# Splitting the first load and the first backward scan of a recurrent attention kernel's boot in two

## The chip, the core and the metric

The kernel runs on one core of a Trainium2 chip. The core has four engines that compute, each with its own list of instructions: TensorE (PE in the profile; PEld is its loading of weights), VectorE (DVE), ScalarE (ACT) and GpSimd (POOL). SyncE (SP) issues most of the DMAs, which move data between the chip's memory and the core's. The metric is the device time of the whole kernel in microseconds, as a median over runs.

## What is computed

The reference is a recurrent attention (RWKV-6) and, on its result, a two-layer network with the activation h - tanh(h):

```python
for t in range(S):                      # B, H, S, D = 4, 8, 768, 48
    kt, vt, rt, wt = (k[:, :, t], v[:, :, t], r[:, :, t], w[:, :, t])
    cur = np.einsum('bhd,bhe->bhde', u[None] * kt, vt)
    y[:, :, t] = np.einsum('bhd,bhde->bhe', rt, state + cur)
    state = wt[:, :, :, None] * state + np.einsum('bhd,bhe->bhde', kt, vt)
x = y.transpose(0, 2, 1, 3).reshape(B * S, H * D)
h = x @ w_in                            # 384 -> 2048
g = h - np.tanh(h)
out = g @ w_out                         # 2048 -> 384
```

The decay w lies between 0.8 and 0.95, one factor for every position and feature. All inputs are float32.

## The kernel before

**Tiles.** The work is cut into eight blocks of 384 positions (four batches, two blocks each). A block has six chunks of 64 positions. The eight heads go in four pairs (numbered 0 to 3); a pair of heads fills the 128 partitions with their features (48 of each 64 used), and positions run along the columns. In w each chunk has 65 columns: a leading one and 64 positions, so a pair of one block has 6 x 65 = 390 columns, and two pairs, a "half" of a block, have 780. The half with pairs 2 and 3 comes first (`h1` in the code), that with pairs 0 and 1 second (`h2`).

**The recurrence as matrix products.** Within a chunk the decay between two positions is a product of w's. Two scans on VectorE make these products. `behind` (line 420, its instruction recorded at line 429) runs backward over w and writes the tile `post`: at each position the product of all decays from there to the end of its chunk. The columns run in reverse, and at the leading column of each chunk the tile `seed` holds a 1, which restarts the product. `before` (line 413, scan at line 417) runs forward and writes `pre`. `take_whole` (line 449) takes the total decay of each chunk out of `post`, and the reciprocal at line 416 turns it over for `before`. Then k is multiplied into `post` (line 443) and r into `pre` (line 436); TensorE forms the scores within a chunk (line 494) and the turned keys (line 517); VectorE copies the scores under a mask (line 502); line 616 gives what each chunk adds to the state, line 631 scans the states over the chunks, and lines 697 and 679 give the attention's result from scores and states.

**The boot.** The first block can hide behind nothing, and `boot` (line 1128) does it by itself, with an order written out by hand: the instructions of TensorE, SP, VectorE and ScalarE stand in the order of the calls. SP issues first the loads: w of pair 3, w of pair 2, k and r of the first half, w of the second half, v, k and r of the second half, then the first two units of the network's weights. For the first block, w is put into the tile `states` (`states0`), so the profile calls these loads `states<-in_wT`. Then VectorE runs `behind` for pair 3 alone, for pair 2 alone, the totals, `before` and the products for the first half, and `behind` for the second half in one scan of 780 columns. TensorE meanwhile does matmuls on an identity matrix whose results nobody reads (lines 305 and 312; `spare=94, ahead=5, late=6` says how many). ScalarE multiplies u into k (line 454), copies results out of PSUM (lines 523, 729) and rebuilds the weights from the two words that each is stored in (line 264, VectorE's part at line 268).

**After the boot** comes the main loop: for each block sixteen steps of the first layer's product (`first`, line 869; matmuls at line 871), the activation and the second layer (lines 950 and 999), with the next block's attention in between. TensorE is handed this work without a break until the end.

**Order of the queues.** SP issues in the order of the calls. Each DMA reports on one of eight semaphores in turn, and its issue waits until the DMA eight before it has landed. The second unit of weights waits besides until line 616 is done.

Of the kernel before, what the change touches and what calls it, by code (L numbers as in the profile page):

```python
# [55 lines left out]
NCH = NB // L  # L56
NCP = NCH // 2
NPAIR = H // 2
LP = L + 1
WIDE = NPAIR * NCH * LP  # L60
HALF = WIDE // 2 + 2
UP = 2
# [64 lines left out]
def kernel(  # L127
# [12 lines left out]
    nc = tc.nc  # L140
# [46 lines left out]
    def draw(names, cols):  # L187
        nc.gpsimd.memset(mask_all[0:L, cols], 1.0)
        for m in names:
# [5 lines left out]
            else:  # L195
# [10 lines left out]
                   in_=start[:, 0:BANK].unsqueeze(1).to_broadcast([P, 2 * NPAIR * NCP * L // BANK, BANK]))  # L206
# [113 lines left out]
    class Block:  # L320
# [40 lines left out]
        def load(self, name, p0=0, n=NPAIR, as_=None):  # L361
# [4 lines left out]
            else:  # L366
# [2 lines left out]
            return nc.sync.dma_start(out=dst.rearrange("d (p t) -> d p t", p=n),  # L369
                                     in_=src.rearrange("p d t -> d p t"))  # L370

        def by_token(self, name):

            return self.tile(name)[:, 0:NCP * DM].rearrange("t (c e) -> t c e", c=NCP)
# [42 lines left out]
            return nc.vector.tensor_tensor_scan(out=self.tile("pre")[:, cols], data0=self.tile("w")[:, cols],  # L417
                                                data1=start[:, 0:n * NCH * LP], initial=0.0, op0=ALU.mult, op1=ALU.add)

        def behind(self, p0, n):  # L420
            a, width, at = p0 * NCH * LP, n * NCH * LP, p0 % UP * NCH * LP
            t = self.half("post", p0, at + width + 1)[:, at:]
            if at + width == UP * NCH * LP:
                nc.gpsimd.memset(t[:, width:], 1.0)

            def back(x):
                return x[:, ::-1]

            return nc.vector.tensor_tensor_scan(  # L429
                out=back(t[:, 0:width]), data0=back(self.tile("w")[:, a:a + width]),  # L430
                data1=back(seed[:, 0:width]), initial=1.0, op0=ALU.mult, op1=ALU.max)
# [696 lines left out]
    def boot(ps, pair, blk, later):  # L1128
        h1, h2 = HALVES
        blk.tiles["w"] = states0  # L1130
        for name, p0, n in (("w", h1 + 1, 1), ("w", h1, 1), ("k", h1, UP), ("r", h1, UP), ("w", h2, UP)):
            blk.load(name, p0, n)
        blk.load_v()
        blk.load("k", h2, UP)
# [1 line left out]
        more_weights(nc.sync)  # L1136

        both = (h1, h1 + 1), (h2, h2 + 1)
        blk.behind(h1 + 1, 1)
        blk.behind(h1, 1)  # L1140
        blk.take_whole(h1, UP)
        blk.totals_by_column(h1)
# [72 lines left out]
    with tc.tile_pool(name="ps_boot", bufs=1, space=PSUM) as ps_boot:  # L1215
        pieces = boot(Turns([scratch(ps_boot)] + ps_a.both), [hp] + acc, blocks[0], blocks[1])
    ps_d = mains.enter_context(tc.tile_pool(name="ps_d", bufs=1, space=PSUM))
    acc += [ps_d.tile([P, BANK], F32, name=f"acc{j}", tag=f"acc{j}") for j in range(1, NB // P)]
    count = const.tile([P, 1], F32, name="count", tag="count")
    ahead_of_h, rest, formed, extra, behind, due, summed = [], [], [], [], [], [], []  # L1220
    held_back, forming, late = [], [], []

# [24 lines left out]
    for i, blk in enumerate(blocks):  # L1247
# [9 lines left out]
        for f in range(NF):  # L1257
# [21 lines left out]
            if not now:  # L1279
                ops = square + converting(pieces, 2)  # L1280
            elif now == 1:
                ops = rest + late + square + converting(pieces, 3)
            elif not i:
                ops = extra + square + (rest + behind + spare if f < 7 else rest[:1] + behind + spare + rest[1:])
            elif forming:
                ops = between(rest, forming[:2]) + square + formed + forming[2:]
                ops = (between(ops, behind) if len(behind) > 2 else ops + behind) + spare
            elif square:
                ops = (between(rest, behind) if len(behind) > 2 else rest + behind) + square + formed + extra + spare
            else:  # L1290
                ops = between(rest + formed, behind + spare)
            for op in ops:
                op()
            rest, behind, formed, forming, held_back = later_ops, [], [], held_back, []
# [23 lines left out]
            if not later and f == NF - 2:  # L1318
                at = n_whole + n_excess
# [29 lines left out]
            for name in loads.get(f, ()):  # L1349
                of, ins = (after if name in ("w", "k", "r") else later), None  # L1350
# [103 lines left out]
```

## Time and profile before

| | us |
|---|---|
| median of 3 runs | 544.92 |
| lowest and highest | 544.65, 544.99 |
| the profiled execution | 545.84 |
| its span, first to last instruction | 544.1 |
| TensorE busy | 533.7 |
| VectorE busy | 459.0 |
| ScalarE busy | 403.8 |

The mean granted clock of TensorE was 0.995 of the full one. The profiled execution has its own time, 545.84, which holds the span and 1.7 us around it. Start times in the profile count from the first instruction. A busy time is the sum of an engine's instructions. The chain that ended last is followed back from the last instruction to what released it, step by step; only what is on it sets the time. A DMA has two times: how long SP was busy with its issue, and how long it was from the issue to the landing of its last byte.

### The profile page before, as it was taken

How to read it: one execution, taken by the hardware profiler on the slowest of the kernel's cores; microseconds unless marked ns; L12 is line 12 of the kernel's file. 1: busy time of each engine (PE TensorE's matmuls, PEld its weight loads, DVE VectorE, ACT ScalarE, POOL GpSimd, SP SyncE). 2: the span in 40 equal slices, each digit the busy share in tenths (PEclk: the TensorE clock that was granted, in tenths of full speed). 3: DMA queues.
4: the chain of work that ended last, by engine and by line, in shares of the span. 5: the costliest groups of instructions: out<-in, count | busy, mean ns of one | idle time of the engine just before them, and what ended most of it. 6: DMA issues, size and time to landing. Idle time of an engine off the chain costs nothing.

```text
span 544.1 us, 14866 instructions
## 1 busy us (share of the span) xinstructions
PE 533.7 (98%) x5682; PEld 404.1 (74%) x5682; DVE 459.0 (84%) x943; ACT 403.8 (74%) x814; POOL 6.6 (1%) x47
## 2 busy tenths in 40 slices
PE   7899999999999999999999999999999999999996
PEld 5756666678887788777877787877878787787874
DVE  7889999999989989789897979879897997457564
ACT  5799996888668876688676886588866885666561
POOL 1100000000000000000000000000000000000000
PEclk9899999999999999999999999999999999999999
DMA  7798633251402631154212532137231420200101
GB/s 274 236 400 308 237 102 115 87 146 60 121 19 79 159 110 54 58 128 138 60 55 73 121 116 67 49 89 161 67 97 54 92 56 2 57 1 0 45 1 46
DMA packets 53048, 56.34 MB, mean 104 GB/s; under 512 B 21488, under 2 KB 50928, under 8 KB 52976
## 3 DMA queue, kind: packets, MB, share of 16 engines
q1 hardware_dynamic: 52592, 55.18, 33.8%
q8 instruction: 48, 0.79, 0.6%
q14 instruction: 24, 0.20, 0.1%
q10 hardware_dynamic: 288, 0.10, 0.1%
q0 software_dynamic: 96, 0.07, 0.1%
HBM read 44.73 MB, written 4.72 MB: 91 GB/s over the span
## 4 chain that ended last, share of the span: by engine, by line
PE 95%; DVE 2%; issue 1%; DMA 0%; PEld 0%; PEldq 0%; DVEq 0%; SPq 0%
PE hp L871 44%; PE acc L999 26%; PE att L999 7%; PE acc L950 5%; PE att L757 4%; PE att L494 2%; PE acc L977 2%; PE att L575 1%; PE att L871 1%; PE acc L871 1%; DVE post L429 1%; DVE scores L502 1%; DMA states<-in_wT 0%; DVE pre L417 0%; PE att L977 0%
## 5 line engine op out<-in xcount | busy, mean ns | idle before, releaser
L871 PE MATMUL hp<-xT,w_sb 128*128 128x384 f32 x738 | 259.2, 487 | 0.4 <-DVE w_sb L268 0.4
L871 PEld LDWEIGHTS hp<-xT,w_sb 128*128 128x128 f32 x738 | 131.9, 190 | 69.7 <-issue 0.5
L999 PE MATMUL acc<-forms,g 128*128 128x128 f32 x954 | 133.2, 276 | 0.0
L876 ACT ACTIVATE h<-hp 128x384 f32<-128x384 f32 x123 | 60.4, 491 | 97.3 <-PE hp L871 97.1
L999 PEld LDWEIGHTS acc<-forms,g 128*128 128x128 f32 x954 | 122.0, 192 | 10.3
L879 DVE SCALAR_TENSOR_TENSOR h<-h,s 128x384 f32<-128x384 f32 x128 | 70.5, 551 | 50.5 <-ACT s L894 50.4
L920 DVE TENSOR_TENSOR g<-g 128x256 f32<-128x256 f32 x265 | 103.1, 418 | 7.3 <-PE acc L999 6.5
L895 ACT ACTIVATE qa<-s,shift 128x384 f32<-128x384 f32 x113 | 69.5, 615 | 3.7
L897 ACT ACTIVATE junk<-s,shift 128x384 bf16<-128x384 f32 x113 | 67.7, 599 | 0.0
L879 DVE SCALAR_TENSOR_TENSOR g<-qa,h 128x384 f32<-128x384 f32 x112 | 61.6, 550 | 1.6 <-ACT qa L905 0.2
L894 ACT ACTIVATE s<-h 128x384 f32<-128x384 f32 x113 | 59.1, 523 | 3.5
L999 PEld LDWEIGHTS acc<-w_sb,g 128*128 128x128 f32 x318 | 46.8, 191 | 9.7 <-ACT sums L967 0.3
L999 PE MATMUL acc<-w_sb,g 128*128 128x128 f32 x318 | 53.1, 276 | 0.0
L999 PE MATMUL att<-w_sb,g 128*128 128x128 f32 x212 | 35.5, 275 | 0.0
L999 PEld LDWEIGHTS att<-w_sb,g 128*128 128x128 f32 x212 | 31.1, 192 | 5.3
L1034 DVE TENSOR_TENSOR sums<-sums 128x256 f32<-128x256 f32 x84 | 32.8, 406 | 1.7 <-ACT sums L1011 1.5
L950 PE MATMUL acc<-w_sb,sums 128*128 128x384 f32 x96 | 33.7, 487 | 0.0
L264 ACT ACTIVATE up<-raw 128x768 f16<-128x768 f32 (+1 forms) x32 | 33.1, 1069 | 0.0
L950 PEld LDWEIGHTS acc<-w_sb,sums 128*128 128x128 f32 x96 | 18.0, 190 | 12.3 <-DVE sums L879 0.3
L417 DVE TENSOR_TENSOR_SCAN pre<-w,start 128x780 f32<-128x780 f32 x14 | 25.0, 1783 | 0.8
L429 DVE TENSOR_TENSOR_SCAN post<-w,seed 128x780 f32<-128x780 f32 x14 | 24.8, 1774 | 0.0
L897 ACT ACTIVATION_READ_ACCUMULATOR junk<-s,shift 128x1 f32 x113 | 21.1, 187 | 0.0
(118 smaller groups left out, 529.2 us busy)
## 6 DMA issues: line engine op xcount, KB each, us to landing
raw<-in_weights SPq DMA_DIRECT2D x16, 768.0 KB, 5.9
w<-in_wT SPq DMA_DIRECT2D x7, 780.0 KB, 4.6
k<-in_kT SPq DMA_DIRECT2D x7, 768.0 KB, 4.6
r<-in_rT SPq DMA_DIRECT2D x7, 768.0 KB, 4.6
v_sb<-in_v SPq DMA_DIRECT2D x8, 576.0 KB, 3.9
k<-in_tokens SPq DMA_DIRECT2D x7, 576.0 KB, 5.2
r<-in_tokens SPq DMA_DIRECT2D x7, 576.0 KB, 4.7
out_y<-sums SPq DMA_DIRECT2D x18, 128.0 KB, 1.8
```

The source lines that it names most:

```text
L264: return lambda: nc.scalar.activation(out=to, in_=of, func=AF.Copy, scale=scale, bias=bias)
L429: return nc.vector.tensor_tensor_scan(out=back(t[:, 0:width]), data0=back(self.tile("w")[:, a:a + width]), data1=back(seed[:, 0:width]), i ...
L871: nc.tensor.matmul(hp, lhsT=w_in_sb[:, f, kc, :], rhs=xT[kc], start=(kc == KC - 1), stop=(kc == 0))
L876: return h, nc.scalar.activation(out=h, in_=hp, func=AF.Copy, scale=1.0 / UPSCALE)
L879: return lambda: nc.vector.scalar_tensor_tensor(out=out, in0=in0, scalar=scalar, in1=in1, op0=op0, op1=ALU.mult)
L894: nc.scalar.activation(out=s, in_=h, func=AF.Square)
L895: nc.scalar.activation(out=qa, in_=s, func=AF.Square, bias=shift[:, 4:5])
L897: nc.scalar.activation(out=junk[:, 0:NB], in_=s, func=AF.Relu, bias=shift[:, 5:6], accum_out=excess[:, at:at + 1])
L920: return lambda: nc.vector.tensor_tensor(out=G[:, to:to + 2], in0=two(G, g_at(q, a0), g_at(q, a1)), in1=two(G, g_at(q, b0), g_at(q, b1)), ...
L950: nc.tensor.matmul(acc, lhsT=g[:, j * P:(j + 1) * P], rhs=w_out_sb[:, f, :], start=(f == self.first), stop=(f == NF - 1))
L999: nc.tensor.matmul(to, lhsT=G[:, g_at(q, a), :], rhs=rhs, start=start, stop=stop, skip_group_check=True)
L1034: ops.append(lambda op=op, at=at: nc.vector.tensor_tensor(out=at[0], in0=at[1], in1=at[2], op=OPS[op]))
```

## The change

The load of w for pair 3 is replaced by two loads of 195 columns each: first chunks 3 to 5 of that pair, then chunks 0 to 2. The backward scan of pair 3, one instruction of 390 columns, becomes two of 195 in the same order (the scan runs backward, so the later chunks come first). Everything else keeps its order. SP has one DMA more ahead of all other loads, VectorE one scan more. Lines behind the change move: 429 becomes 434, 449 becomes 454, 502 becomes 507, 697 becomes 702 and so on; the new loads are on line 374.

```diff
+        def load_chunks(self, p, chunks):
+            at, of = (slice((n + chunks.start) * LP, (n + chunks.stop) * LP) for n in (p * NCH, self.q * NCH))
+            return nc.sync.dma_start(out=self.tile("w")[:, at], in_=wT[self.b, p, :, of])
...
-        def behind(self, p0, n):
-            a, width, at = p0 * NCH * LP, n * NCH * LP, p0 % UP * NCH * LP
+        def behind(self, p0, n, chunks=slice(0, NCH)):
+            first, last = (p0 * NCH + c for c in (chunks.start, (n - 1) * NCH + chunks.stop))
+            a, width, at = first * LP, (last - first) * LP, first % (UP * NCH) * LP
...
     def boot(ps, pair, blk, later):
         h1, h2 = HALVES
         blk.tiles["w"] = states0
-        for name, p0, n in (("w", h1 + 1, 1), ("w", h1, 1), ("k", h1, UP), ("r", h1, UP), ("w", h2, UP)):
+        parts = slice(NCP, NCH), slice(0, NCP)
+        for part in parts:
+            blk.load_chunks(h1 + 1, part)
+        for name, p0, n in (("w", h1, 1), ("k", h1, UP), ("r", h1, UP), ("w", h2, UP)):
             blk.load(name, p0, n)
...
-        blk.behind(h1 + 1, 1)
+        for part in parts:
+            blk.behind(h1 + 1, 1, part)
         blk.behind(h1, 1)
```

## The prediction

> **What bounds the kernel now.** I read the page first: the totals and the chain that ended last.
>
> ```profile
> span 544.1 us, 14866 instructions
> ...
> PE 533.7 (98%) x5682; PEld 404.1 (74%) x5682; DVE 459.0 (84%) x943; ACT 403.8 (74%) x814; POOL 6.6 (1%) x47
> ...
> PE 95%; DVE 2%; issue 1%; DMA 0%; PEld 0%; PEldq 0%; DVEq 0%; SPq 0%
> ```
>
> TensorE holds 95% of the chain. The change adds nothing to it, so only what starts TensorE's long run earlier or later can count. Hence the second view: the chain in order of time, first 40 us (start, length, what).
>
> ```profile
> 0.94 2.60 DMA states<-in_wT
> ...
> 3.64 1.84 DVE post L429 x2
> ...
> 7.77 0.32 DVE post L443
> ...
> 8.62 0.95 DVE pre L436
> ...
> 12.31 0.16 DVE post L443
> ...
> 13.17 1.03 DVE scores L502
> ...
> 14.24 0.59 PEld att L697 x36
> ...
> 25.02 4.98 PE acc L871 x12
> 30.01 1.94 PE hp L871 x6
> ```
>
> Here the change sits on the path: the chain begins with the first load of w (tile `states`), goes on with the two backward scans of line 429, and stays on VectorE until line 697 hands it to TensorE. A tenth gained or lost there is a tenth of the whole, if nothing between takes it back. What could take it back are the other loads of the boot, so the third view is SP's timeline (start, length of the issue), and behind it the time from issue to landing: by tile, w then k then r, minimum/median/maximum, and then one row for each load.
>
> ```profile
> 0.94 0.87 SPq L369 DMA_DIRECT2D states<-in_wT  x2
> 1.86 0.43 SPq L369 DMA_DIRECT2D k<-in_kT  x1
> 2.33 0.48 SPq L369 DMA_DIRECT2D r<-in_rT  x1
> 2.85 0.47 SPq L369 DMA_DIRECT2D states<-in_wT  x1
> 3.37 0.48 SPq L406 DMA_DIRECT2D v_sb<-in_v  x1
> 3.89 0.76 SPq L369 DMA_DIRECT2D k<-in_kT  x1
> 4.69 0.92 SPq L369 DMA_DIRECT2D r<-in_rT  x1
> 5.65 8.21 SPq L251 DMA_DIRECT2D raw<-in_weights  x2
> ```
>
> ```profile
> DMA to landing us min/median/max: 2.6/2.7/6.2
> ...
> DMA to landing us min/median/max: 5.2/6.7/8.1
> ...
> DMA to landing us min/median/max: 5.7/7.0/8.3
> ```
>
> ```profile
> raw<-in_weights SPq DMA_DIRECT2D x1, 768.0 KB, 9.2
> v_sb<-in_v SPq DMA_DIRECT2D x1, 576.0 KB, 7.6
> ...
> u_sb<-in_uT ACTq DMA_DIRECT2D x1, 2.0 KB, 2.2
> ```
>
> Start plus landing time gives: pair 3 of w 0.94 + 2.6 = 3.54; pair 2 of w 1.39 + 2.7 = 4.09 (its issue is the second of the two in 0.87 us); k 7.06; r 8.03; w of the second half 2.85 + 6.2 = 9.05; v 10.97; k of the second half 3.89 + 8.1 = 11.99; r of the second half 12.99; the first weights 5.65 + 9.2 = 14.85. The first scan starts at 3.64, 0.10 after its load: that is the price from landing to start. It does not wait for pair 2, so a scan waits for its own load alone.
>
> **The front end, step by step.** The rows for a scan's length and for the rate of transfer (the window row reads: length, busy time of the engines, clock, DMA share, GB/s):
>
> ```profile
> L429 DVE TENSOR_TENSOR_SCAN post<-states,seed x3: 944/971/1775, 3.6 to 9.5; 128x390 f32<-128x390 f32 x2, 128x780 f32<-128x780 f32 x1
> ```
>
> ```profile
> 2.50:3.50 1.00, 1.00 (x47) 1.00 (x44) 0.00 (x0) 0.99 (x3) 0.64 (x3) 1.00 0.99 347
> ```
>
> - Landing of a half. 195 KB land in 2.6, 2 KB in 2.2. The ends for 97.5 KB are these two; in the middle lies 2.4, which I take. The first half lands at 3.34, its scan starts at 3.44: a lead of 0.20 (0 to 0.40).
> - Scan of 195 columns. From 390 to 780 columns it costs 1775 - 944 = 831 ns more, 2.13 ns a column; so 195 columns cost 944 - 415 = 0.53 us, between half of 944 (0.47) and 944. The line through two rows is near the lower end, so I take 0.53. The halves together are 1.06 where one scan had 0.92 of the chain (1.84 / 2): 0.14 of the lead is gone.
> - Second half. An issue slot is (2.33 - 0.94) / 3 = 0.46. Issued at 1.40, landed at 3.80, usable at 3.90; the first scan ends at 3.97. No wait.
> - Pair 2. This is the step the lead dies on. Its load is now third, at 0.94 + 2 x 0.46 = 1.87. With the best landing time of a load its size, 2.6, it lands at 4.47 and its scan starts at 4.57. The two halves are done at 3.44 + 1.06 = 4.50. Before, the same scan started at 3.64 + 0.92 = 4.56. So the pair of scans ends at 4.57 + 0.92 = 5.49, where it was 5.48: the front end gives nothing, +0.01. A half's issue could be shorter than a slot; no row shows a load of w of such size, and the two k issues, one size, took 0.43 and 0.76, so I leave it a slot. If the issues of both halves fit in one slot, and the lead is 0.40, and the halves cost 0.92 together, the scans end at 5.08: -0.40.
>
> The Trainium skill, "DMA: Bandwidth & Descriptors", section "Anatomy of one DMA", speaks against halving: about 2.0 us of a DMA are fixed and only bytes over 436 GB/s scale, for DMAs issued from GpSimd. By it a half would land 0.23 earlier, an estimate from that page, beside my 0.20; the rows 2.2 and 2.6 agree with it, and the sum would not move.
>
> **The queue behind it.** Every later load of the boot is issued one slot (0.46) later. What of this reaches the landing? At 347 GB/s 195 KB (199,680 bytes) take 0.575 us. Before, two w loads kept the queues busy for 1.15, longer than their two slots (0.93): k started 1.15 after the first byte. After, the pair 2 load has its slot at 0.93 and is done at 1.50; three slots are 1.39. So k, and all behind it, comes 1.50 - 1.15 = 0.35 later (bounds: 0, if the later backlog swallows the hole, and 0.57, below). What each load has to spare is read from these rows (VectorE's, TensorE's and ScalarE's timeline):
>
> ```profile
> 9.49 1.77 DVE L429 TENSOR_TENSOR_SCAN post<-states,seed 128x780 f32<-128x780 f32 x1
> ...
> 11.39 1.02 DVE L502 COPY_PREDICATED scores<-mask_all,att 128x768 f32<-128x768 uint8 x1
> ```
>
> ```profile
> 12.19 0.25 PE L616 MATMUL hp<-v_sb,ks 64*64 64x48 f32 x1
> ```
>
> ```profile
> 14.98 0.90 ACT L264 ACTIVATE w_sb<-raw 128x768 f32<-128x768 f32 x1
> 16.54 0.97 ACT L729 COPY late<-att 48x384 f32<-48x384 f32 x2 [0.66 <-PE att L679]
> ```
>
> - k is used at 7.77, has 7.77 - 7.06 - 0.10 = 0.61 to spare; r at 8.62, 0.49; w of the second half at 9.49, 0.34; v at 12.19, 1.12. Three are covered for 0.35, and the w load is even (0.01 late).
> - k of the second half is used at 12.31, where VectorE comes from the scores of 11.39 (no wait now): spare 12.31 - 11.99 - 0.10 = 0.22. **Here 0.35 - 0.22 = 0.13 comes out.** Queued behind that product on VectorE is the masking copy at 13.17, and line 697 on TensorE waits for that.
> - r of the second half (12.99) is used only after line 697's matmuls, over a microsecond later: free.
> - The first weights slip to 15.20 and ScalarE converts until 16.20 instead of 15.88; its idle 0.66 before 16.54 hides that. Without that idle it would cost 0.32.
> - Loads also wait in SP for the load eight before them, as the program lists them: k of the second half now for u (0.90 + 2.2 = 3.1), r for the first half of w (3.34), the first weights for the second half (3.80). All are landed before the issue, at 4.35 and later. The second weights wait for line 616, as before; later loads keep their partner.
> - GpSimd's memset of line 424 stays one per half tile; one VectorE instruction is added, counted above.
>
> Sum: the path is late by the larger of +0.01 (front end) and +0.13 (k of the second half), so +0.13. The profiled execution was 545.84 (span 544.1, 1.7 around it), and would be 545.97; it stands 0.92 above the median of 544.92, which would be **545.05**.
>
> **The rivals.**
> 1. *The lead comes through.* The half's issue is short, or the backlog swallows the hole. For it: the queues are not starved from 5 us on, when landing times are 5 to 8 us. Against: pair 2 needs its own 2.6. Even with no slip at all, k of the second half is usable at 12.09, so at most 12.31 - 12.09 = 0.22 is gained: 544.70.
> 2. *A packet of 780 bytes costs what one of 1560 does.* Then a half takes 0.575, as does a whole load: three make 1.725, the slip is 0.57. The first scan gets no lead (3.64 to 4.17), the second half lands at 4.11 (4.21 to 4.74), pair 2 lands at 4.68, its scan runs from 4.78 to 5.70; k of the second half is usable at 11.99 + 0.57 + 0.10 = 12.66: +0.35, 545.27.
> 3. *A second clock cut: slower.* TensorE's granted clock was halved once, right behind the boot (columns as above, TensorE's busy time first, the clock third from the end):
>
> ```profile
> 16.60:20.01 3.41, 3.03 (x138) 2.48 (x134) 3.38 (x4) 3.36 (x6) 1.58 (x3) 1.00 0.28 87
> 20.01:23.42 3.41, 2.28 (x67) 2.14 (x67) 2.85 (x7) 2.53 (x3) 0.13 (x2) 1.00 0.87 269
> 23.42:26.84 3.42, 3.35 (x51) 2.52 (x52) 1.77 (x4) 2.21 (x4) 0.00 (x0) 0.50 0.96 350
> ```
>
> ```profile
> 14.24 0.90 PE L697 MATMUL att<-scores,v_sb 64*48 64x64 f32 x48
> ...
> 23.49 1.53 PE L697 MATMUL att<-scores,v_sb 64*48 64x64 f32 x48 [0.24 <-DVE w_sb L268]
> ```
>
> The cut lasted 3.42 us and cost 1.53 - 0.90 = 0.63 on line 697 and 4.98 - 2 x 1.94 = 1.10 on the first twelve matmuls of line 871: 1.73. It followed a stretch of the same length in which TensorE worked 2.28, in narrow matmuls. The stretch before that had 3.03. If the boot slips so that 0.75 more idle falls into that one, a second cut would come: 544.92 + 1.73 = 546.65. My slip of 0.13 is far from it.
> 4. *The cut goes.* The same price the other way: 543.19, if the shifted boot fills the stretch before 23.42. The idle there belongs to steps that shift together, which speaks against it. The Trainium skill, "TensorE: Matmul & The Clock Gate", Part 1, says that the activity window is 3413 ns and free-running, not tied to the kernel's start; the length of 3.42 here agrees. By it a cut would come and go from one execution to the next in both kernels alike, and the median would not move for it; no run here shows that yet.
>
> **How the numbers follow.** Forecast 0.60; rival 1 0.14; rival 2 0.16; rival 3 0.06; rival 4 0.04. About 0.2% (1.09 us) is what a measurement of this kernel can tell from no change. The forecast and rivals 1 and 2 lie within it: same 0.90. Rival 4 is the faster 0.04, rival 3 the slower 0.06. The range reaches from rival 1's 544.70 to rival 2's 545.27, widened on each side by about 0.2 for the spread of the runs shown (544.65 to 544.99): 544.5 to 545.5. It leaves out rivals 3 and 4, 0.10, and their like.
>
> **What would show it.** Two scans of 195 columns near 0.53 us each, the first from about 3.44; the scan of pair 2 again at 4.5 to 4.6 with a short wait for its load, the first total (line 454 in the changed file) where it was, near 5.5; k of the first half landing 0.2 to 0.5 later; a small new wait of VectorE for the second half's k near 12.4; line 697's matmuls (now 702) near 14.4 instead of 14.24; the clock halved once for 3.4 us. I am wrong if the pair 2 scan starts before 4.4 (the issue is cheaper), if the second half's k does not slip, or if the number or place of the clock cuts differs.

## The result, and the profile after

| | us |
|---|---|
| after, median of 22 runs | 545.58 (544.72 to 548.87) |
| before, median of 22 runs beside them | 544.66 (543.61 to 547.26) |
| ratio of after to before | 1.0027, 95% interval 1.0015 to 1.0039 |
| forecast | 545.05, range 544.5 to 545.5 |
| profiled execution after: time, span | 545.66, 543.9 |
| profiled execution before: time, span | 545.84, 544.1 |

The change makes the kernel slower: by 0.92 us between the medians, and by 0.27% in the ratio, which is not formed from the two medians. The forecast was +0.13 us. The two profiled executions hide this: that of before is the longer one. So the totals of the profile can't be compared, and the stages must be. First the page's head for the kernel after:

```profile
span 543.9 us, 14868 instructions
...
PE 533.7 (98%) x5682; PEld 403.1 (74%) x5682; DVE 459.4 (84%) x944; ACT 403.7 (74%) x814; POOL 6.6 (1%) x47
```

Every engine is as busy as it was; VectorE has one instruction more (944). Why the profiled execution of before is long is seen in the stretch that rival 3 quoted (after; length, busy times, then clock, DMA share and GB/s):

```profile
23.42:26.84 3.42, 3.17 (x56) 1.93 (x55) 2.49 (x6) 2.57 (x5) 0.00 (x0) 1.00 0.98 341
```

The granted clock was 0.50 here before and is 1.00 now. That execution of before paid the cut, 1.73 us by the prediction's sum; this one of after did not.

**The boot.** VectorE's timeline of after, from the first scan (start, length, idle time and what ended it):

```profile
3.12 0.57 DVE L434 TENSOR_TENSOR_SCAN post<-states,seed 128x195 f32<-128x195 f32 x1 [1.53 <-DMA states<-in_wT]
4.88 1.52 DVE L434 TENSOR_TENSOR_SCAN post<-states,seed 128x195 f32<-128x195 f32 x2 [1.20 <-DMA states<-in_wT]
6.43 0.17 DVE L454 TENSOR_SCALAR whole<-post 128x12 f32<-128x12 f32 x1
...
7.01 1.78 DVE L421 TENSOR_TENSOR_SCAN pre<-states,start 128x780 f32<-128x780 f32 x1
```

The first half's scan starts at 3.12, 0.52 earlier than the scan of before (3.64). Then VectorE waits 1.20 for the second half, and the group of two that starts at 4.88 (the second half's scan and pair 2's) ends at 6.40. The first total starts at 6.43; before it was 5.50. **The boot is 0.93 late at this point.** The halves themselves cost what they should: 0.57 for the first, and in the trace 0.56 for the second.

The loads of the first 3 us in after (KB each, median us from issue to landing), and the range for the two halves:

```profile
k<-in_kT SPq DMA_DIRECT2D x1, 384.0 KB, 4.1
r<-in_rT SPq DMA_DIRECT2D x1, 384.0 KB, 4.7
states<-in_wT SPq DMA_DIRECT2D x2, 97.5 KB, 2.8
states<-in_wT SPq DMA_DIRECT2D x1, 195.0 KB, 3.5
```

```profile
DMA to landing us min/median/max: 2.1/2.8/3.5
```

The first half took 2.1 and the second 3.5, though they are alike and were issued 0.45 apart; pair 2's load took 3.5 where the two loads of its size took 2.6 and 2.7 before. From the trace the three landed at 3.02, 4.86 and 5.41. Meanwhile k, next in SP's queue behind pair 2, took 4.1, where it took 5.2 before (the minimum of k's row in the prediction): it landed at 2.33 + 4.1 = 6.43 instead of 7.06. So it looks as if what held k up before now holds up the loads of w. The rate of all transfers fits this. Each figure is 0.08 us, from 2.40 to 5.60; before first, then after:

```profile
GB/s 196 255 314 392 449 312 371 312 429 332 351 331 331 253 271 173 96 96 115 192 96 230 230 250 326 211 269 269 230 211 230 211 211 192 269 288 403 307 326 288
```

```profile
GB/s 342 351 215 215 254 224 215 127 127 58 78 78 117 136 214 292 312 351 292 155 97 155 39 173 298 385 318 327 269 327 269 288 327 288 307 384 365 307 365 307
```

Before, the rate falls from about 330 to 173 and then to about 100 from 3.60 on (the 16th figure) and partly recovers, to above 200, from 4.08 (the 22nd). By then both loads of w are nearly through (the second lands at 4.07), and k pays. After, it falls below 130 at 2.96 (the 8th figure) and recovers from 3.5, with a second fall near 4: now the second half and pair 2 are on their way, and they pay. I call this **the dip** below.

The same slices of after, now with the mean busy share of the 16 engines that move the data, in tenths:

```profile
DMA  9988799994675357899969147989797888999999
```

At 2.96 and 3.04 (the 8th and 9th figures) the engines are still at 9 while the rate has fallen to 127. From 3.12 to 3.44 they are at 4, 6, 7, 5 and 3, about half, and the rate is about a quarter of what it was. So in the dip transfers take longer, and besides fewer of them are under way.

The chain of waits of after, from the boot's part of the whole chain (start, length, what), must be read with care:

```profile
2.82 4.69 DMA r<-in_rT
...
7.56 1.15 issue
8.71 0.93 DVE post L448
9.64 0.87 DVE pre L441
10.51 1.70 DVE post L434
```

It names r's load instead of w's. But r landed at 7.51, and for 1.15 behind it the chain has only "issue": VectorE's timeline above says what it did then, the scan of line 421 from 7.01 to 8.79. That scan follows the late total; r's landing set nothing.

In this execution the delay stays whole as far as line 702 (start, length):

```profile
15.17 0.90 PE L702 MATMUL att<-scores,v_sb 64*48 64x64 f32 x48
```

It starts at 15.17, where line 697 started at 14.24: +0.93 again.

**The end.** The last work on the chip is the store that ScalarE issues. For before: its issue on ScalarE's timeline, the DMA row with its size and its time to landing, and SP's row of waits (in total, how often, the longest):

```profile
540.12 0.36 ACTq L983 DMA_DIRECT2D out_y<-g  x1
```

```profile
out_y<-g ACTq DMA_DIRECT2D x1, 96.0 KB, 2.4
```

```profile
SPq L1386 <- SPq L1386: 1.9, 3, 1.1
```

The same three views for after:

```profile
539.07 0.36 ACTq L988 DMA_DIRECT2D out_y<-g  x1
```

```profile
out_y<-g ACTq DMA_DIRECT2D x1, 96.0 KB, 2.7
```

```profile
SPq L1395 <- SPq L1395: 2.7, 1, 2.7
```

Before, the store lands at 540.12 + 2.4 = 542.52 and the span ends at 544.1, 1.58 later. After, it lands at 539.07 + 2.7 = 541.77 and the span ends at 543.9, 2.13 later (with all digits of the trace 1.572 and 2.117). **That is +0.54 at the very end, with nothing left to hide it.** The rows of waits say how: the kernel closes with a row of eight waits of SP, one for each of the eight semaphores on which the DMAs report in turn, always in the same order. Before, the last store reports on the eighth: SP is through the other seven when it lands, its last wait is the longest (1.1), and only what follows the eight waits is left, 1.54 in both kernels. After, with one DMA more in the program, the last store reports on the first: SP sits in its first wait for 2.7 and then has seven more to go through, though all are over. In the trace the first ends at 541.84 and the eighth at 542.39, about 0.08 for each.

Boot and end together would give 0.93 + 0.54 = 1.47 if nothing behind line 702's first matmuls took any of it back. Between these two executions something does: TensorE idles 1.22 at 19.75 in before and 0.67 at 20.55 in after (rows "issue" of the two chains, no cause shown), and the second batch of the line starts at 23.73, only 0.24 later than at 23.49. In e2 and e3 below, which have the loads of before and no such gap, that batch starts at 22.80 and 22.96. So for this stage too the profiled execution of before was a long one.

The medians differ by 0.92, the fastest executions by 1.11, and the ratio of 1.0027 on 544.66 is 1.47. That the last figure equals the sum is no confirmation, since 5 of the 22 executions of after had a lower granted clock (below). That the causes are these two, and how large each is, the experiments must say.

### The profile page after: what moved, and what is told of

It reads as the page before. It is cut to its first block, busy times and chain, and to the rows that moved or that the text cites. A ratio compares the mean times of both kernels' runs of the same rounds, so it can differ in the third digit from the quotient of the medians.

```text
span 543.9 us, 14868 instructions
## 1 busy us (share of the span) xinstructions
PE 533.7 (98%) x5682; PEld 403.1 (74%) x5682; DVE 459.4 (84%) x944; ACT 403.7 (74%) x814; POOL 6.6 (1%) x47
## 4 chain that ended last, share of the span: by engine, by line
PE 94%; DVE 2%; issue 1%; DMA 1%; PEld 0%; SPq 0%; PEldq 0%; DVEq 0%
PE hp L876 44%; PE acc L1004 27%; PE att L1004 7%; PE acc L955 5%; PE att L762 4%; PE att L499 2%; PE acc L982 2%; PE att L580 1%; PE att L876 1%; DMA r<-in_rT 1%; PE acc L876 1%; DVE pre L421 1%; DVE pre L441 0%; DVE post L434 0%; PE att L982 0%
```

## The experiments

**The theories.** A, *the end*: one DMA more turns the order of the eight semaphores and costs 0.54, whatever the boot does. B, *the boot*: the loads of pair 3's halves make pair 2's load late, 0.3 to 0.9 of it reaches the end. Rivals: the second scan itself costs time; rows of 780 bytes are slow; the order of the loads matters, not their size. In the table "first total" is the start of the first total on VectorE, "line 697" the start of that line's first matmul (line 702 in after), "end" the time from the last landing to the end of the span; the four times are from the trace of one execution. The difference is that of the medians on the same chip.

| run | pair 2 lands | first total | line 697 | end | difference | ratio, 95% interval |
|---|---|---|---|---|---|---|
| before | 4.07 | 5.50 | 14.24 | 1.57 | | |
| after | 5.41 | 6.43 | 15.17 | 2.12 | +0.92 | 1.0015 to 1.0039 |
| e8, the change again | 4.88 | 5.90 | 14.64 | 2.12 | +0.56 | 1.0002 to 1.0027 |
| e1, the change, end turned back | 4.77 | 5.80 | 15.38 | 1.59 | +0.24 | 1.0000 to 1.0018 |
| e2, only the end turned | 4.10 | 5.54 | 14.39 | 2.12 | +0.45 | 0.9997 to 1.0015 |
| e3, only the scan halved | 4.09 | 5.58 | 14.59 | 1.57 | +0.31 | 0.9991 to 1.0009 |
| e4, only the load halved | 4.97 | 6.00 | 14.73 | 1.60 | +0.61 | 1.0002 to 1.0020 |
| e5, halves by rows | 5.24 | 6.27 | 15.01 | 1.60 | +0.80 | 0.9997 to 1.0032 |
| e6, unread half load between | 5.49 | 6.52 | 15.27 | 1.59 | +0.94 | 1.0010 to 1.0035 |
| e7, second half from ScalarE | 4.80 | 5.83 | 14.57 | 1.60 | +0.08 | 0.9991 to 1.0010 |
| e9, one load for both pairs | 4.26 | 6.22 | 14.97 | 1.57 | +0.55 | 1.0004 to 1.0035 |
| e10, second half behind pair 2 | 3.97 | 5.45 | 14.79 | 1.60 | +0.35 | 0.9984 to 1.0019 |
| e16, pair 2 from ScalarE | 4.21 | 5.90 | 14.63 | 1.59 | +0.43 | 1.0001 to 1.0018 |

Five more had one execution each; they are read by their traces alone.

### The two causes apart: e1, e2, e8

e1 is the change with the same number of DMAs on the eight semaphores as before: a load late in the kernel, of a row that is needed much later, is issued by GpSimd, whose DMAs take no turn on them (e11 below shows it).

```diff
-                    ins = nc.sync.dma_start(out=u_row, in_=u_all)
+                    ins = nc.gpsimd.dma_start(out=u_row, in_=u_all)
```

> The whole change, with one later load (u for a whole row, needed late) issued by GpSimd instead of SP, so that the count of loads on the shared completion semaphores is that of before again. Lane theory: the end gets its old form, the last wait of the closing row right behind the landing of the last store (0.04 us in before, 0.58 in the changed kernel), and the time is about 0.55 below the changed kernel, 0.0 to 0.4 above before. Boot theory: the first total again near 6.4 us instead of 5.5, and if the whole loss of 0.9 is the boot's, the time stays 0.9 above before. If the late landing of the second half was chance, the first total comes at 5.4 to 5.6.

e2 is the kernel before with that same load cut in two on SP: one DMA more on the semaphores, the boot untouched.

```diff
-                    ins = nc.sync.dma_start(out=u_row, in_=u_all)
+                    nc.sync.dma_start(out=u_row[:, 0:DM // 2], in_=u_all[:, 0:DM // 2])
+                    ins = nc.sync.dma_start(out=u_row[:, DM // 2:], in_=u_all[:, DM // 2:])
```

> Before, with one load in the main loop (u for a whole row) cut in two, so that one DMA is added far from the boot. Lane theory: boot as before (first total near 5.5), the last store is waited for first of eight, and the waits behind it add 7 x 0.085 = 0.6 us: 0.4 to 0.7 above before. Boot theory: no difference to before, within 0.2.

e8 is the changed kernel again, unaltered.

> The changed kernel itself once more, for a second look at its boot and for its time on the chip of the three others. Boot theory: pair 2 landed later than 4.6, first total between 5.7 and 6.5. Lane theory: 0.54 between the landing of the last store and the last of the eight end waits beyond what before has. Time 0.5 to 1.4 above before.

SP's closing waits in e1, then in e2:

```profile
SPq L1395 <- SPq L1395: 1.9, 3, 1.0
```

```profile
SPq L1387 <- SPq L1387: 2.4, 1, 2.4
```

e1, with the change in it, has the waits of before (three, the longest 1.0) and an end of 1.59; e2, without the change, has those of after (one long wait first) and an end of 2.12. So the 0.54 comes with the number of DMAs and from nothing in the boot. Theory A fits every trace: the end is 2.12 with one DMA more, and 1.57 to 1.60 with as many as before. In time, e2 lies 0.45 above before; its ratio's interval reaches from -0.16 to +0.82 us and thus holds 0.54, and also nothing. Among the executions with a granted clock of 0.997 or more, e2's mean is 0.42 above that of before (95% interval about 0.1 to 0.7).

e1 and e8 show the boot. VectorE's timeline of e1, then of e8:

```profile
3.15 0.57 DVE L434 TENSOR_TENSOR_SCAN post<-states,seed 128x195 f32<-128x195 f32 x1 [1.57 <-DMA states<-in_wT]
4.24 1.52 DVE L434 TENSOR_TENSOR_SCAN post<-states,seed 128x195 f32<-128x195 f32 x2 [0.52 <-DMA states<-in_wT]
5.80 0.17 DVE L454 TENSOR_SCALAR whole<-post 128x12 f32<-128x12 f32 x1
```

```profile
3.13 1.02 DVE L434 TENSOR_TENSOR_SCAN post<-states,seed 128x195 f32<-128x195 f32 x2 [1.54 <-DMA states<-in_wT]
4.90 0.97 DVE L434 TENSOR_TENSOR_SCAN post<-states,seed 128x390 f32<-128x390 f32 x1 [0.75 <-DMA states<-in_wT]
5.90 0.17 DVE L454 TENSOR_SCALAR whole<-post 128x12 f32<-128x12 f32 x1
```

In e8 the second half is there in time, and VectorE waits 0.75 for pair 2. In e1 and in after VectorE waits for the second half (0.52 and 1.20), and pair 2 lands (4.77 and 5.41) just as that half's scan ends: either load alone would have made the delay. The same boot loses 0.30, 0.40 or 0.93 by the first total, from one execution to the next. e1's first total was expected near 6.4, or at 5.4 to 5.6 if the late landing had been chance; 5.80 is neither.

The first total is not the last word. In e1 VectorE waits twice more, for r of the first half (landed at 9.12) and for w of the second half (10.59):

```profile
9.21 0.96 DVE L441 TENSOR_TENSOR pre<-r,pre 128x768 f32<-128x768 f32 x1 [0.21 <-DMA r<-in_rT]
10.62 1.78 DVE L434 TENSOR_TENSOR_SCAN post<-states,seed 128x780 f32<-128x780 f32 x1 [0.45 <-DMA states<-in_wT]
```

So its line 702 starts 1.14 later than line 697 in before, the largest delay in the table. The same w of the second half is waited for in e10 (0.50, landed at 10.00) and, with the very loads of before, in e3 (0.17, landed at 9.80). By the medians the change costs +0.24 with the end turned back and +0.56 or +0.92 as it is; e1 and e2 add up to 0.69, between these. The spread of one boot from execution to execution is as large as what is to be explained.

### Which half of the boot's edit: e3, e4

e3 keeps the one load and halves the scan; e4 halves the load and keeps one scan of 390 columns, with line 1363's load from GpSimd as in e1.

```diff
-        blk.behind(h1 + 1, 1)
+        for part in parts:
+            blk.behind(h1 + 1, 1, part)
```

> Only the scan of pair 3 in two, the load whole. Step of the prediction: a half costs 0.53, two of them 0.14 more than one; the first total at 5.64 instead of 5.50; time 0.0 to 0.14 above before. Boot theory in which the loads do the harm: the same. A scan whose cost is mostly fixed: first total at 6.0 or later.

```diff
-        for part in parts:
-            blk.behind(h1 + 1, 1, part)
+        blk.behind(h1 + 1, 1)
...
```

> Only the load of pair 3 in two (the scan of 390 columns waits for both halves), the later load of u from GpSimd so that the end keeps its form. If the load in two does the harm in the boot: the scan starts at 4.8 to 5.0, the first total comes near 6.7, time 0.3 to 0.6 above before (some of the 1.2 comes back later, as in the changed kernel). By the prediction's sums: second half landed at 3.8, scan from 3.9, pair 2 from 4.82, first total at 5.76, time up to 0.3 above before.

The scans of e3 on VectorE's timeline, three of them in one group:

```profile
3.66 1.88 DVE L434 TENSOR_TENSOR_SCAN post<-states,seed 128x195 f32<-128x195 f32 x3 [2.08 <-DMA states<-in_wT]
5.58 0.17 DVE L454 TENSOR_SCALAR whole<-post 128x12 f32<-128x12 f32 x1
```

Three scans take 1.88 where two took 1.84 in before's chain. The first total is 0.08 later, 0.02 of it from a later landing, and no difference in time is shown (+0.31 between the medians, but a ratio of 1.0000, 0.9991 to 1.0009). e4 has the late boot without the second scan (first total 6.00) and is slower. Its second half landed at 3.67, earlier than either of its expectations, and its scan starts at 3.79; pair 2 alone, at 4.97, makes it late. So it is the load, not the scan.

### What about the load: e5, e6, e7

e5 cuts pair 3's load by partitions instead of columns (two loads of 64 rows of 1560 bytes). e6 puts a half load that nobody reads between the whole load of pair 3 and that of pair 2. Both have line 1363's load from GpSimd. e7 issues the second half from ScalarE at 0.90 and u from GpSimd, so that SP issues pair 2 in its old slot.

```diff
-        for part in parts:
-            blk.load_chunks(h1 + 1, part)
+        for rows in (slice(0, 64), slice(64, P)):
+            blk.load_rows(h1 + 1, rows)
...
```

> The load of pair 3 in two by partitions, 64 and 64, each row its full 1560 bytes; the scan whole, waiting for both; the end's form kept by the later load of u from GpSimd. To be held against the columns in two with a whole scan (pair 2 landed at 4.97, first total 6.00). If short rows of 780 bytes do the harm: pair 2 landed at 4.4 to 4.5, first total 5.6 to 5.75. If it is the third place in the queue behind two small loads, whatever their rows: pair 2 landed at 4.8 or later, first total 5.9 or later.

```diff
+        blk.load("w", h1 + 1, 1)
+        nc.sync.dma_start(out=unread, in_=wT[blk.b, h1 + 1, :, 0:NCP * LP])
...
```

> Before, load and scan of pair 3 whole, with a load of 195 columns into a tile that nobody reads between the loads of pair 3 and pair 2; the end's form kept. Pair 2 is the third issue as in the changed kernel, but with more bytes ahead. If only the slot counts: pair 2 landed at 4.4 to 4.5, first total at 5.50 to 5.55, time within 0.3 of before. If queues that run dry between small loads do the harm: the same, since 195 KB fill them. If a third load is slow to start in itself: pair 2 landed at 4.8 to 5.4, first total 5.8 to 6.4, time 0.3 to 0.9 above before.

```diff
-    nc.scalar.dma_start(out=u_sb, in_=uT)
+    nc.scalar.dma_start(out=states0[:, 3 * NCH * LP:(3 * NCH + NCP) * LP], in_=wT[0, 3, :, 0:NCP * LP])
...
```

> The change, but the second half of pair 3 is issued by ScalarE as its first DMA (where u was), u comes from GpSimd, and SP keeps the slots of before; as many DMAs on the shared semaphores as before. If SP's extra slot is what eats the lead: both halves landed by 3.3, pair 2 by 4.1 to 4.2, first total 5.1 to 5.3, time 0.2 to 0.4 below before. If two small loads ahead of it slow pair 2 whoever issues them: pair 2 landed at 4.5 or later, first total 5.5 or later.

e5 has no short row and still lands pair 2 at 5.24. A part of that is its longer issues (1.22 for the two loads of 64 rows), which put pair 2's at 2.20; but from there it took 3.04, not 2.6. So rows of 780 bytes are not the cause. Rival 2 of the prediction falls by the first half already, which gave the lead that it denied (first scan at 3.12 in after). e6 has the loads of before, whole, and one more half load between them; pair 2 took 3.63 from its issue at 1.86 and landed at 5.49, later than any of e6's expectations. The transfer rate of e6, from 2.40 in steps of 0.08:

```profile
GB/s 157 177 256 392 411 361 380 361 303 234 185 205 166 68 20 20 78 0 98 234 254 176 195 175 136 174 272 329 367 348 348 308 288 327 403 384 422 403 384 365
```

The dip comes from 3.4 to 3.9, and at its bottom nearly nothing moves. e7 gives pair 2 its old slot (1.39) and it still lands at 4.80, 0.73 later than before, so the slot alone isn't it either. Its first total and its line 702 are 0.33 late, yet no loss of time is shown (+0.08, from -0.49 to +0.54 by the interval).

### Order and amount: e9 to e13, e15, e16

e9 loads both pairs with one DMA; e10 moves the second half behind pair 2 in loads and scans; e11 is the kernel before with one DMA less on the eight semaphores.

```diff
-        for name, p0, n in (("w", h1 + 1, 1), ("w", h1, 1), ("k", h1, UP), ("r", h1, UP), ("w", h2, UP)):
+        for name, p0, n in (("w", h1, UP), ("k", h1, UP), ("r", h1, UP), ("w", h2, UP)):
```

> Before, with the loads of pair 3 and pair 2 in one DMA of 390 KB (k is then the second load), the scans as before, and one later load cut in two so that the end keeps its form. If the third load of the queue is the slow one: k lands at 4.5 to 5.5 and r is slow to start. If the slow patch lies in time, from about 3 us on, whatever the count: k, the second load, is the slow one, landed at 6.0 to 7.0 as in before. Both scans wait for the one load, landed near 4.1, first total 6.0 to 6.1, time 0.3 to 0.6 above before.

```diff
+        blk.load_chunks(h1 + 1, parts[0])
+        blk.load("w", h1, 1)
+        blk.load_chunks(h1 + 1, parts[1])
...
```

> The change with pair 2 second and the second half of pair 3 third, loads and scans both, the end's form kept. Pair 2 second: landed at 4.0 to 4.2 as in before. If the third place is slow: the half lands at 4.4 to 5.0 though it has 97.5 KB, and the first total is at 5.5 to 5.7. By the prediction's sums the half would land at 1.87 + 2.4 = 4.3 and the total come at 4.17 + 0.92 + 0.53 = 5.62 or a little after. Time within 0.3 of before.

> Before with the later load of u issued by GpSimd, so one DMA less on the shared semaphores: the last store is waited for seventh of eight. Lane theory: the span ends 1.58 + 0.07 = 1.65 us after the landing of the last store (1.58 in before, 2.12 in the changed kernel). A third look at the boot of before besides: pair 2 landed at 4.1, first total 5.5.

e9's one load lands at 4.26, so its first scan starts 0.72 later than before's. But its rate, from 2.40 in steps of 0.08, has no dip behind the first load, and k, issued at 1.46, landed 3.8 later, at 5.29. It is r, the third load here, that is late: it landed at 7.38, 2.10 behind k, where its bytes at 347 GB/s take 1.13. The rate:

```profile
GB/s 78 21 98 195 292 332 390 410 332 351 448 410 370 389 466 348 366 403 422 384 403 365 326 442 403 384 365 365 327 288 250 288 307 211 288 269 307 365 365 327
```

e10 lets the pieces land in the order 2.98, 3.97, 4.20, so its third load is not slow (2.35 from its issue), and VectorE shows the lead at last:

```profile
3.08 0.57 DVE L434 TENSOR_TENSOR_SCAN post<-states,seed 128x195 f32<-128x195 f32 x1 [1.50 <-DMA states<-in_wT]
3.99 1.42 DVE L434 TENSOR_TENSOR_SCAN post<-states,seed 128x390 f32<-128x390 f32 x2 [0.35 <-DMA states<-in_wT]
5.45 0.17 DVE L454 TENSOR_SCALAR whole<-post 128x12 f32<-128x12 f32 x1
```

Its first total is at 5.45, as early as in e11 (5.45), whose boot is that of before: of 0.56 of lead, 0.35 is waited away for pair 2 and the rest goes on the second scan. So even with the loads in good time the split brings nothing by the first total, and further on e10 is 0.55 late at line 702, mostly by its wait of 0.50 for w of the second half. e11's time was 544.97 and its end 1.66: the last store now reports on the seventh semaphore, and one wait follows it. By the end it is 0.08 worse than before, which stood at the best place already.

Five runs asked why pair 2 is late. e12 puts a load of 2 KB ahead of all; e15 (and e15b, the same again) puts it between pairs 3 and 2; e13 puts a whole load of 195 KB there; e16 is e1 with pair 2's load issued by ScalarE. The first four are made from before, with the late load from GpSimd; the added loads are read by nobody.

> Before with a load of 2 KB (16 bytes a row) ahead of all others on SP, into a tile that nobody reads; the end's form kept. Pair 2 is third by count, but with no more bytes ahead. If a third load is slow to start: pair 2 landed at 4.9 to 5.5, first total 5.9 to 6.5. If the slow patch follows time: pair 2, one slot later at 1.87, falls into its beginning, landed at 4.7 to 5.2. If it follows the bytes moved: pair 2 landed at 4.5 to 4.6, first total 5.9 to 6.0 (the first scan starts at 4.1), and k is slow.

```diff
+        blk.load("w", h1 + 1, 1)
+        nc.sync.dma_start(out=unread, in_=uT)
...
```

> The kernel before, with a 2 KB load that nobody reads between pair 3 and pair 2 of w, and line 1357's load from GpSimd. The same loads as in the run with the 2 KB load first (there pair 2 took 2.58 us, landed 4.44), only in another order: now 0.575 us of bytes are followed by a load of next to nothing, and the queues run dry from about 0.6 to 0.93 after the first byte. Theory 'dry queues': pair 2 takes 2.9 to 3.6 us from issue, lands 4.8 to 5.5, first total 5.8 to 6.5. Rival 'only the issue slot counts': 1.86 + 2.6 = 4.46, first total 5.5 to 5.55.

> The same kernel once more, for the spread of one look. Both theories expect what they expect of the first: 'dry queues' pair 2 landing at 4.8 to 5.5, 'only the slot' near 4.46.

```diff
+        blk.load("w", h1 + 1, 1)
+        nc.sync.dma_start(out=unread, in_=wT[blk.b, h1 + 1, :, 0:NCH * LP])
...
```

> The kernel before, with one more load between pair 3 and pair 2 of w that nobody reads, 390 columns like theirs (pair 3's rows again, 195 KB), and line 1357's load from GpSimd, so that the end of the kernel is as before. Pair 2 is the third load, issued near 1.86, while 0.575 us of bytes of the load ahead are still to come, so the queues never run dry. Theory 'a load that comes to dry queues is slow': pair 2 here takes about 2.6 to 2.8 and lands near 4.5 to 4.75, first total 5.5 to 5.8. Rival 'the third load, or one more load ahead, is slow whatever its size' (change and unread-load run: 3.0 to 3.6 us): pair 2 lands at 5.0 or later, first total 6.0 or later.

```diff
     nc.scalar.dma_start(out=u_sb, in_=uT)
+    nc.scalar.dma_start(out=states0[:, 2 * NCH * LP:3 * NCH * LP], in_=wT[0, 2, :, 0:NCH * LP])
...
```

> The change (load and scan of pair 3 in halves) with the load of w for pair 2 issued by ScalarE, right behind its load of u (issue near 1.34), and line 1363's load from GpSimd, so that the end is as before; SP then issues both halves, k, r and the rest in the slots that it had before. Bytes and rows are those of the change. Theory 'SP's own queue stalls once, on its load that follows the first two or three': k, SP's third load, takes the stall as in the kernel before (k near 7.0), and pair 2, on ScalarE's queue, lands 2.6 to 3.0 after its issue, at 4.0 to 4.4; first total 5.2 to 5.5; time 0.0 to 0.3 below the kernel before. Rival 'the stall comes after the first loads, whichever queue issues what follows': pair 2 lands at 4.8 or later, first total 5.8 or later, time 0.2 to 0.6 above the kernel before.

The rates, from 2.40 in steps of 0.08: e12 (2 KB first), e15 (2 KB between), e13 (195 KB between), e16.

```profile
GB/s 117 78 117 117 136 156 292 254 312 370 312 254 371 332 312 390 468 389 292 212 116 38 77 96 134 154 192 403 326 307 384 346 346 403 384 327 326 403 346 307
```

```profile
GB/s 98 176 280 414 296 300 197 216 177 126 43 39 98 156 78 156 234 273 292 331 310 310 426 328 346 308 327 307 307 346 288 307 288 422 307 288 288 269 346 307
```

```profile
GB/s 117 177 261 375 391 351 351 390 390 410 371 370 332 312 254 195 156 98 156 58 136 59 20 39 117 117 175 156 253 234 175 252 251 173 250 289 288 288 288 365
```

```profile
GB/s 334 351 273 205 137 136 156 98 185 224 390 361 400 371 350 360 338 299 356 307 442 269 269 307 269 365 365 365 384 288 250 288 230 269 269 250 288 326 346 403
```

e12 has pair 2 as its third load, and it took 2.58 from its issue (landing 4.44, nearest to what was expected if the slow patch follows the bytes moved); the dip comes at 4.0, behind it. With the very same loads in another order, e15, the dip comes at 3.1, behind pair 3, and pair 2 landed at 4.98 (again: 4.90), 3.1 from its issue. So neither the count nor the slot makes it late. Both executions of e15 are as "dry queues" expected: a load is slow when nothing was left to move ahead of it. **e13 refutes this**: there 195 KB stand ahead of pair 2, the dip comes all the same, from 3.7 to 4.6, and pair 2 landed at 5.74. Nor is a third load slow whatever its size, as e13's rival has it: e12's and e10's were not. e16 refutes both of its own expectations in part: ScalarE's load of pair 2 landed in 2.87, at 4.21, as "SP's own queue" said, but SP's k was not late (5.50); the dip came at 2.7 and the second half paid, at 4.41, so the first total is 5.90 again.

What the other boots shown here have in common is this: the rate falls to a third or less, for 0.4 to 1 us, near the end of the first loads. (e10, whose rate isn't shown, has two falls, to 98 at 2.8 and to 19 at 4.1.) It falls at 2.7 to 3.0 with two halves ahead on SP (after, e16), at 3.1 to 3.4 with a whole load and a smaller one (e15, e6), at 3.6 to 4.0 with two whole ones (before, e13, e12). Less work ahead brings it forward, and what is then on its way is late. e9, where the same 390 KB came as one load instead of two, is the boot without a dip: so it may belong to the seam between loads rather than to bytes, but no run tried that by itself, and a load is late there all the same. All this is a description; why the rate falls stays open.

## Why the prediction was wrong

**The step that failed in the boot is "Pair 2".** It took the best landing time of its size, 2.6, and got 4.47; measured were 5.41 (after), 4.88 (e8) and 4.77 (e1), 2.9 to 3.5 from the issue. A minimum over loads that were issued ahead of the dip was used for one behind it. The row that spoke against it was quoted: k, third in before, took 5.2 for 384 KB, which at 347 GB/s are 1.13. Behind the second load of w (4.09) it was due at 4.09 + 1.13 = 5.22 and landed at 7.06: 1.84 went unexplained, and the prediction took it as k's own. (Three other executions with the loads of before, e2, e3 and e11, had k at 6.35, 6.25 and 6.12: still about 1 late.) In the runs the delay fell on whichever load was on its way behind the first ones. In the forecast's sum the front end was +0.01; it is +0.93 in after, +0.40 in e8, +0.30 in e1. "Second half" failed with it in two of the three: it was to land at 3.80 and not be waited for, and landed at 4.86 in after and 4.22 in e1 (3.34 in e8). e7 shows that even the old slot would not have saved pair 2.

**The step that failed at the end is "only what starts TensorE's long run earlier or later can count".** The added DMA counts behind that run as well. The step on semaphores ("Loads also wait in SP for the load eight before them ... later loads keep their partner") asked only who waits at an issue. It did not follow their turn to the kernel's last line, where their order costs 0.54 (1.57 to 2.12). The forecast put this term at nothing.

**"Landing of a half".** The first half landed at 3.02 to 3.06, not 3.34: 2.1 from its issue, and the lead of the first scan was 0.52, not 0.20, and outside the bounds of 0 to 0.40. The lower bound was u's 2.2 for 2 KB, and u itself took 1.9 in after. The Trainium skill, "DMA: Bandwidth & Descriptors", section "Anatomy of one DMA", would by its rule, stated for DMAs issued from GpSimd, have a half 0.23 earlier than a whole load, an estimate from that page; the traces say 0.52 (3.54 against 3.02) for these loads of SP, so here that rule is too small by 0.29.

**"Scan of 195 columns".** Right: 0.57 and 0.56 in after against 0.53 each. The 0.14 for two was more than enough; e3 loses 0.08 at the first total.

**"The queue behind it".** k and all behind it were to come 0.35 later. Against before's profiled execution, k and r of the first half and w of the second came 0.54 to 0.63 earlier (k at 6.43 against 7.06), while v, k and r of the second half and the first weights came 0.28 to 0.30 later (second half's k at 12.27 against 11.99). One pair of executions does not settle the sign: with the loads of before, e2, e3 and e11 had k at 6.12 to 6.35 and the second half's k at 12.16 to 12.34. The wait for the second half's k, the forecast's whole 0.13, did not come, because VectorE itself was 0.93 late: in after the mask of line 507 starts at 12.32 and the product of line 448 at 13.24, with no wait between. Where a later load did stall VectorE (e1, e3, e10, e12), it was w of the second half, which this step had as even, and in e1 r of the first half too. So that the sign of the whole came out as forecast is luck: the +0.13 was to come from a wait that after doesn't have. The slots of 0.46 were right.

**The clock, rivals 3 and 4.** A cut comes in some executions of either kernel: in after 5 of 22 executions had a granted clock of 0.992 to 0.994 and took 547.3 to 548.9, and before has such executions too (0.992 to 0.995 at 545.6 to 548.0 in the runs beside the experiments). The Trainium skill, "TensorE: Matmul & The Clock Gate", Part 1, says that the window of 3413 ns is free-running. The traces agree: the first change of the clock that they record lies at 6.36 (before), 9.65 (after), 6.66 (e2), 7.51 (e8) and 10.85 us (e6), and the cut of before lies 17.07 behind it, five times 3.413. So neither rival is shown to belong to the change. Whether a boot that is 0.9 late meets the cut more often, the runs are too few to tell.

**The range** was built from bounds on the front end of 0 to -0.40, with nothing above +0.2 but rival 2's. A dip of which before shows one place gave no bound on what it would cost at another; e8 would have fallen inside (545.19 beside a before of 544.63), but 545.58 did not. That a measurement tells only about 0.2% from no change no run shows: here 22 executions of each told 0.27%, with an interval from 0.15% to 0.39%.

How much of the boot's delay reaches the end is bounded only. By the start of line 697 or 702, 0.49 goes with +0.61 in e4, 1.03 with +0.94 in e6, 0.55 with +0.35 in e10 and 0.35 with +0.31 in e3, but 0.33 with +0.08 in e7 and 1.14 with +0.24 in e1: the start is from one execution, the time from ten or more. TensorE's gaps around line 494 vary by up to a microsecond between executions (1.22 at 19.75 in before, none in e2, e3 and e8), so a single one can't settle it to a tenth.

## What to carry to other kernels

Ahead of a split of an early load, ask which load the next transfer's delay will fall on, and read it from the load that stands in that place now, not from the best of its size. Read the landings of several executions, since one boot's loads moved by half a microsecond and more between them. Count the DMAs when an edit adds one: where a kernel's end waits for its semaphores in a fixed order, the place of the last store in it is worth half a microsecond, and a load of no importance can be moved to another issuer to set it. A profile that is faster than that of before proves nothing where one cut of the clock costs more than the change.

## What the hardware showed that was not expected

The eight closing waits cost about 0.08 us each even when nothing is left to wait for; the last store on the first, seventh and eighth semaphore landed 2.12, 1.66 and 1.57 us ahead of the span's end. In the boots shown here, but for e9's, the transfers fall from over 300 GB/s to below 130, with nearly nothing moving at the bottom in e6 (0 to 20 GB/s), and the fall comes sooner the less is loaded ahead of it. A load of 2 KB moved ahead of two whole loads instead of between them changed the landing of the second from 4.98 to 4.44.
